# Attention and a gated feed-forward network on one core: pairs of logits emitted by free banks instead of fixed slots, other durations in the planner, and dense work dealt out differently

## The chip, the cores and the metric

The kernel runs on one NeuronCore of a Trainium2 chip. The core has a matrix engine (TensorE, "PE" in the profile), three engines for element-wise work (VectorE "DVE", ScalarE "ACT", GpSimd "POOL"), a queue engine (SyncE "SP") and 16 DMA engines. TensorE writes into PSUM, which has eight banks of 128 x 512 float32. The metric is the device time of one execution in microseconds.

## The reference

Two branches read the same input x (2048 tokens x 640) and are mixed by a gate that depends on the token:

```python
g = sigmoid((x * gate_w).sum(-1, keepdims=True))
out = g * A(x) + (1 - g) * B(x)
```

B is a feed-forward network, `(silu(x @ w1) * (x @ w3)) @ w2` with 1728 hidden columns. A is attention with a memory, 32 heads of 20 columns, the tokens in four chunks of 512:

```python
for s in range(4):                     # chunks
    logits = qs @ ks.T * scale + mask  # mask: (key > query) * -1e9
    a_dot = softmax(logits) @ vs
    a_mem = (phi(qs) @ M) / (phi(qs) @ z + 1e-6)
    o = sigmoid(beta) * a_mem + (1 - sigmoid(beta)) * a_dot
    M += phi(ks).T @ vs ; z += phi(ks).sum()
out_A = concat(o) @ wo
```

Everything is float32.

## The kernel before

**Precision.** A float32 operand is split into a high and a low part of type float32r (`split`, `parts`, `split_psum`), and three products (high x high, high x low, low x high; `PASSES`) stand for one. ScalarE makes the high part, VectorE or GpSimd the low part. A few small products (the memory's `pm` and `nd`, and the product of the probabilities with the values, `o`) use plain float32.

**Two halves of the array.** Nearly all matmuls use 64 of TensorE's 128 rows. `halves` cuts the 128-deep sum of a tile into a part for rows 0 to 63 (r = 0) and one for rows 64 to 127 (r = 1); while one tile does its first part on half 0, an older tile does its second part on half 1. Logits are made for two heads at once, one on each half.

**The planner.** The Python source writes the order of all engines by hand: an instruction runs on its engine in the order in which the source emits it. To choose this order the source keeps a clock of its own. `put(r, ns)` adds a matmul's duration to the clock of its half, `clocks[r]`; `go(engine, ns)` adds to that engine's time, `busy`; `until[bank]` is the time at which a PSUM bank is empty again. `stages` emits a chain of instructions on several engines, each when the one before is done by this clock. The durations are constants in the source: `COL` (0.4533 ns a column) for float32r matmuls, `COL4` for float32 ones, `MIN_MM` as a floor.

**Dense work.** A `Work` is one PSUM tile: its matmuls and the function that empties it (`evac`). Dense work is written as generators of `Work`: projections q, k and v; `ffn_up` (g and u), `ffn_down` (f, a sum over a group of three hidden blocks); the output projection (op); the memory (`pkt`, `pm`, `nd`); the normalisation of the attention's output (`rr`, `gt`). `step` emits one matmul, of the half whose clock is behind. `under` holds tiles on their first half, `behind_one` tiles that wait for their second, `flight` the one on it. `braid` runs one generator as a `Side` of another: it gives a tile every so many nanoseconds of dense work.

**Attention.** `attention()` walks through slots, 40 for a quad of heads (two pairs). `S_AT` and `T_AT` name the slots in which a pair's logits are made: `s_unit` makes them queries by keys for the row maxima (VectorE, L981), `max_rows` sends the maxima back into the operands by DMA, `t_unit` makes them again, transposed, with the maxima in, for the exponentials (ScalarE, L1026, into P) and masks (GpSimd, L1035). `pv_quad` multiplies P by the values (o, L1052); the last row of o is the sum of the probabilities. A unit takes two banks with `take_bank`; if none is free by the source's clock, the clock is moved on. `o_sums` and `o_scale` turn a chunk's sums into factors: one DMA brings them to `rs`, six VectorE instructions make reciprocals in three bfloat16 parts `rp`, six DMAs bring these into `rR`, and `rr` matmuls spread them over the output's rows.

**Segments.** `segs` lists dense jobs with the slot at which they must be done: 0 (the FFN of chunks 0 and 1, after the projections in `head`), 1, 2, 3 and 4. Within a segment the loop at the end of the kernel deals out dense work evenly over its slots. What remains after the last slot is `tail`: a down projection for group 3 of chunks 2 and 3, the last group, and the output projection of chunk 3.

## Time and profile before

| | us |
|---|---|
| median of 3 runs | 1137.55 (1133.83 to 1139.9) |
| the profiled execution's own time | 1137.45 |
| its span, first to last instruction | 1135.7 |
| TensorE busy | 1106.9 |
| VectorE, GpSimd, ScalarE busy | 582.5, 552.0, 485.6 |

The mean granted TensorE clock is 0.993. A row of the groups reads: line, engine, operation, out<-in by the program's names, partitions x elements, count, then busy time, mean duration in ns, and the idle time of the engine just before these instructions with what ended it. The names are those of the kernel: g, u, f, op, q, k, v are dense tiles; s and t the two kinds of logits; o the product with the values; P the probabilities; W and ht split weights and hidden blocks. "PE" rows are matmuls, "PEld" rows weight loads. A timeline row begins with its start and its duration in us, and ends with the idle time before it.

### The profile page before, as it was taken

To read this page: it belongs to the slowest core of one execution; us is meant where nothing else is said; L and a number is where in the kernel's file an instruction comes from. 1 tells how busy PE (TensorE), PEld (TensorE's weight loads), DVE (VectorE), ACT (ScalarE), POOL (GpSimd) and SP (SyncE) were. 2 spreads that over 40 slices of the span, in tenths; PEclk is the share of its full clock that TensorE was granted. 3 is DMA by queue.
4 is the path that set the end of the run, shared out by engine and by line. 5 is a ranking of instruction groups with operands and counts; after the bars stand their busy time and mean duration, and the time that the engine had idled before them with its cause. 6 is when DMAs were issued, how large, how long until landed. Compare 5 with 4: busy or idle time off the path is not lost. (4 is left out here: it accounts for less than half of the span.)

```text
span 1135.7 us, 29817 instructions
## 1 busy us (share of the span) xinstructions
PE 1106.9 (97%) x11798; PEld 988.7 (87%) x11798; DVE 582.5 (51%) x1735; ACT 485.6 (43%) x1003; POOL 552.0 (49%) x739
## 2 busy tenths in 40 slices
PE   9999999999999999999999989999999999999998
PEld 6999998988888998889989878888788888886998
DVE  6032564355555544473344666663457674652553
ACT  5255334543352433355456634535442445245130
POOL 5444356455464545334445445555663657464230
PEclk9999999999999999999999999999999999999999
DMA  7456753334343423614477863426533434452111
GB/s 258 149 195 223 250 153 95 88 93 113 90 115 91 105 54 98 197 48 140 158 257 244 270 212 94 122 84 194 152 99 93 121 95 116 119 142 65 41 67 62
DMA packets 85883, 152.34 MB, mean 134 GB/s; under 512 B 19914, under 2 KB 33009, under 8 KB 85745
## 3 DMA queue, kind: packets, MB, share of 16 engines
q1 hardware_dynamic: 55569, 94.13, 25.9%
q0 software_dynamic: 22976, 41.90, 15.3%
q10 hardware_dynamic: 7200, 14.42, 3.4%
q8 instruction: 93, 1.52, 0.6%
q14 instruction: 45, 0.37, 0.1%
HBM read 94.92 MB, written 54.53 MB: 132 GB/s over the span
## 5 line engine op out<-in xcount | busy, mean ns | idle before, releaser
L251 PE MATMUL g<-X,W 64*128 64x512 f32 x1680 | 390.9, 397 | 0.1
L251 PE MATMUL u<-X,W 64*128 64x512 f32 x1560 | 373.9, 397 | 0.0
L981 DVE CUSTOM_DVE_ANT_0 junk<-s,mask 128x128 bf16<-128x128 f32 (+3 forms) x512 | 250.9, 490 | 201.2 <-PE s L970 164.9
L1026 ACT ACTIVATE P<-t 128x384 f32<-128x384 f32 (+1 forms) x384 | 180.4, 526 | 247.4 <-PE t L1019 235.0
L251 PEld LDWEIGHTS g<-X,W 64*128 64x128 f32 x1680 | 271.9, 186 | 15.2 <-issue 2.0
L167 POOL TENSOR_TENSOR W<-wr,W 128x640 fp32r<-128x640 f32 (+1 forms) x125 | 195.3, 1569 | 162.6 <-ACT W L171 156.5
L251 PE MATMUL f<-W,ht 64*128 64x320 f32 x2624 | 268.3, 311 | 5.0 <-POOL ht L880 3.4
L251 PEld LDWEIGHTS u<-X,W 64*128 64x128 f32 x1560 | 259.0, 187 | 14.4 <-issue 1.8
L251 PEld LDWEIGHTS f<-W,ht 64*128 64x128 f32 x2624 | 249.2, 187 | 10.4 <-POOL ht L880 5.1
L1035 POOL TENSOR_SCALAR_AFFINE_SELECT P<-P 128x256 f32<-128x256 f32 (+1 forms) x192 | 94.4, 496 | 256.1 <-ACT P L1026 217.5
L171 ACT CAST W<-wr 128x640 fp32r<-128x640 f32 (+1 forms) x130 | 91.5, 727 | 49.2 <-PE f L251 20.5
L1019 PE MATMUL t<-qk 62*128 62x256 f32 (+2 forms) x512 | 99.6, 335 | 7.1 <-DVE m L981 4.6
L251 PE MATMUL op<-W,oT 64*128 64x320 f32 x960 | 99.6, 310 | 2.1 <-DVE oT L167 2.0
L970 PE MATMUL s<-qk 60*128 60x256 f32 (+2 forms) x512 | 94.5, 328 | 3.7 <-ACT P L1026 1.8
L918 DVE SCALAR_TENSOR_TENSOR acc<-f,cgate,acc 128x320 f32<-128x320 f32 x128 | 69.9, 549 | 52.7 <-PE f L251 52.2
L251 PE MATMUL k<-X,W 64*128 64x512 f32 x600 | 95.9, 397 | 0.4 <-SPq L254 0.4
L251 PEld LDWEIGHTS op<-W,oT 64*128 64x128 f32 x960 | 91.2, 186 | 4.3 <-DVE oT L167 3.4
L1006 POOL DMA_DIRECT2D qk<-mr x128 | 73.5, 576 | 35.7 <-DVE mr L1000 30.4
L880 POOL TENSOR_TENSOR ht<-ft,ht 128x512 fp32r<-128x512 f32 x52 | 67.1, 1289 | 48.5 <-ACT ht L884 41.6
L251 PE MATMUL q<-X,W 64*128 64x512 f32 x540 | 86.8, 395 | 0.0
L251 PE MATMUL v<-W,X 64*128 64x320 f32 (+1 forms) x960 | 82.8, 307 | 0.0
L251 PEld LDWEIGHTS k<-X,W 64*128 64x128 f32 x600 | 79.3, 185 | 3.3 <-SPq L254 1.1
(117 smaller groups left out, 1305.5 us busy)
## 6 DMA issues: line engine op xcount, KB each, us to landing
qk<-qkd POOLq DMA_DIRECT2D x128, 240.0 KB, 3.9
wr<-in_w_dram SPq DMA_DIRECT2D x80, 320.0 KB
qkd<-qs SPq DMA_DIRECT2D x20, 512.0 KB
qkd<-ks SPq DMA_DIRECT2D x20, 512.0 KB
od<-oq ACTq DMA_DIRECT2D x32, 256.0 KB
wr<-in_wo_dram SPq DMA_DIRECT2D x20, 320.0 KB
vg<-vd SPq DMA_DIRECT2D x16, 336.0 KB
xr<-in_xT_dram SPq DMA_DIRECT2D x20, 256.0 KB
```

What stands on the lines that cost most here:

```text
L167: (nc.vector if lo else nc.gpsimd).tensor_sub(dst[:, 1], src, dst[:, 0].bitcast(F32))
L171: stages(bank, ("act", ns, lambda: nc.scalar.copy(dst[:, 0], src)), ("dve" if lo else "pool", 1.1 * ns if lo else 2.2 * ns, low))
L251: ins = nc.tensor.matmul(o, l, x, start=i == 0 and (r == 0 or not w.todo[0]), stop=i == len(todo) - 1 and (r == 1 or not w.todo[1]), skip_ ...
L880: nc.gpsimd.tensor_sub(ht[:, 1], t, ht[:, 0].bitcast(F32))
L918: nc.vector.scalar_tensor_tensor(dst, ps[:, :320], cgate[:, c, lb:lb + 1], dst, op0=ALU.mult, op1=ALU.add)
L970: nc.tensor.matmul(ps[i][:, o:o + n], q[:, qb * P:(qb + 1) * P], k[:, :n], start=qb != 1, stop=qb != 0, skip_group_check=True)
L981: nc.vector.tensor_tensor_reduce(out=junk[:, :n], in0=ps[i][:, o:o + n], in1=mask[:, L - n:], scale=1.0, scalar=-3.0e38, op0=ALU.add, op1= ...
L1006: after(3 + 9 * k + a, lambda d=dst, r=r: here(nc.gpsimd.dma_start(d, mr[r:r + 8])))
L1019: nc.tensor.matmul(ps[i][:, o:o + L - q0], k[:, kb * P:(kb + 1) * P], q[:, q0:], start=kb != 2, stop=kb != 3, skip_group_check=True)
L1026: nc.scalar.activation(u["P"][:, i, o:o + n], ps[i][:, b:b + n], AF.Exp, scale=SCALE)
L1035: nc.gpsimd.affine_select(d, d, pattern=[[0, 2], [0, n], [1, P]], base=0, channel_multiplier=-1, compare_op=ALU.is_ge, fill=0.0)
```

## The change

`s_unit` and `t_unit` are no longer called in their slots. The slot puts them into a list `units`, and `events`, called after each dense matmul, takes the first from it when three banks are free by the source's clock, or two when the unit is more than `LATE` = 3 slots late; after 6 slots it is emitted anyway, and `flush` empties the list where something needs it. Side jobs open only with three free banks and VectorE's time less than 1 us ahead. A matmul of the second half may go before a new tile is opened when no bank is free, by up to `AHEAD`. Durations are changed, and GpSimd's DMA issues get 580 ns each (`ISSUE`). `o_scale` becomes a chain of stages. The output projection's tiles wait for the part of oT that they read. Dense jobs are moved between segments, and once the segments are used up the loop takes work from the tail.

```diff
-COL, COL4, MIN_MM, APART = 0.4533, 1.667, 110, 5
+COL, COL4, MIN_MM, APART, ISSUE, AHEAD = 0.4533, 0.85, 62, 5, 580, 1000
...
+LATE = 3
...
-               ("dve" if lo else "pool", 1.1 * ns if lo else 2.2 * ns, low))
+               ("dve" if lo else "pool", 1.4 * ns if lo else 2.15 * ns, low))
...
+    def free(n):
+        return sum(t <= now() for t in until) >= n
...
     def events():
 
         due()
+        if units and (free(3) or units[0][0] + LATE < clock["slot"] and free(2)):
+            unit()
...
-            elif dense["ns"] >= d.due and len(under) < 2 and len(behind_one) < 3:
+            elif dense["ns"] >= d.due and len(under) < 2 and len(behind_one) < 3 and free(3) and busy["dve"] < now() + 1000:
...
-        if flight[0] is not None and (clocks[1] < clocks[0] or run is None and not under and not waiting):
+        if flight[0] is not None and (clocks[1] < clocks[0] + (0 if under or free(1) else AHEAD)
+                                      or run is None and not under and not waiting):
...
             if not lower():
-                raise RuntimeError("nothing makes " + waiting[0].name + " ready")
+                if not heap:
+                    raise RuntimeError("nothing makes " + waiting[0].name + " ready")
+                force()
...
         queue.dma_start(raw[:, :n], src)
+        if queue is nc.gpsimd:
+            go("pool", ISSUE)
...
         while i not in tiles:
-            if i in halfway:
+            if i >= clock["oldest"] + NW:
+                if not lower():
+                    raise RuntimeError("no room for weight " + str(i))
+            elif i in halfway:
                 force()
...
-                until[bank] = go("act", 420 if hf == 0 else 700)
+                until[bank] = go("act", 430 if hf == 0 else 660)
...
+    def row_in(u, dst, src):
+        nc.gpsimd.dma_start(dst, src)
+        go("pool", ISSUE)
+        u["in"] = u.get("in", 0) + 1
...
     def max_rows(p):
 
+        flush(lambda: all(f is t_unit or q > p + 1 for _, f, q, _ in units))
         while min(pairs[p + k].get("rows", 0) for k in range(2)) < 6:
             force()
...
-                    after(3 + 9 * k + a, lambda d=dst, r=r: here(nc.gpsimd.dma_start(d, mr[r:r + 8])))
+                    after(3 + 9 * k + a, row_in, pairs[p + k], dst, mr[r:r + 8])
...
     def t_unit(p, t):
 
         u = pairs[p]
+        while u.get("in") != 2:
+            if not soon:
+                force()
+            tick()
...
-                go("pool", 500)
+                go("pool", 430 if n == 1 else 640)
...
     def o_scale(c):
 
-        here(nc.vector.reciprocal(rs, rs))
-        nc.vector.tensor_scalar(rs, rs, cR, None, op0=ALU.mult)
-        nc.vector.tensor_copy(rp[:, 0], rs)
-        nc.vector.tensor_sub(rs, rs, rp[:, 0])
-        nc.vector.tensor_copy(rp[:, 1], rs)
-        nc.vector.tensor_sub(rp[:, 2], rs, rp[:, 1])
-        go("dve", 2200)
-        end = c == NSEG - 1
-        for i in range(3):
+        def send(i):
             for k, (base, h0, n) in enumerate(((0, 0, R1H + 1), (64, R1H, H - R1H))):
                 dst = rR[base + n * i:base + n * i + n].rearrange("h (a n) -> h a n", n=P)
-                queue = nc.gpsimd if end and k else nc.sync
-                after(3 + 2 * i if end else 3 + 2 * i + k,
-                      lambda d=dst, s=rp[4 * h0:4 * h0 + 4 * n, i], q=queue: here(q.dma_start(d, s)))
-        after(11, turned.append, c)
+                queue = nc.gpsimd if k else nc.sync
+                after(1 + k, lambda d=dst, s=rp[4 * h0:4 * h0 + 4 * n, i], q=queue:
+                      (q.dma_start(d, s), q is nc.gpsimd and go("pool", ISSUE)))
+
+        def last():
+            send(2)
+            after(6, turned.append, c)
+
+        def keep(i):
+            return "dve", 240, lambda: nc.vector.tensor_copy(rp[:, i], rs)
+
+        def rest(i):
+            send(i)
+            nc.vector.tensor_sub(rs if i == 0 else rp[:, 2], rs, rp[:, i])
+
+        stages(None, ("dve", 950, lambda: nc.vector.reciprocal(rs, rs)),
+               ("dve", 320, lambda: nc.vector.tensor_scalar(rs, rs, cR, None, op0=ALU.mult)),
+               keep(0), ("dve", 300, lambda: rest(0)), keep(1), ("dve", 300, lambda: rest(1)), ("dve", 0, last))
...
+    def unit():
+
+        _, f, p, t = units.popleft()
+        even()
+        f(p, t)
+
+    def flush(ready):
+
+        while units and not ready():
+            unit()
+
     def attention():
...
-                even()
+                clock["slot"] += 1
                 if n == 2 and 0 <= m - 2 < NQUAD:
+                    flush(lambda: all(p > 2 * m - 3 for _, f, p, _ in units if f is t_unit))
+                    even()
                     pv_quad(2 * m - 4)
                 if n in S_AT and 0 <= m < NQUAD:
                     i, x = S_AT[n]
-                    s_unit(2 * m + i, x)
+                    units.append((clock["slot"], s_unit, 2 * m + i, x))
                 if n in T_AT and 0 <= m - 1 < NQUAD:
                     i, x = T_AT[n]
-                    t_unit(2 * m - 2 + i, x)
+                    units.append((clock["slot"], t_unit, 2 * m - 2 + i, x))
...
-                    load_pair(2 * (m + 1) + (n > 28))
+                    p = 2 * (m + 1) + (n > 28)
+                    flush(lambda: all(q % NST != p % NST for _, _, q, _ in units))
+                    load_pair(p)
+                if units and (units[0][0] + 2 * LATE < clock["slot"]):
+                    unit()
...
             def parts(ps):
-                assert qb in ready, (c, qb)
-                return halves([lambda kb=kb, a=a, b=b: (ps[:, :320], oT[0][:, qb % 2, a, kb * P:(kb + 1) * P],
+                def left(a, kb):
+                    while (qb, KB if kb > 1 else 2) not in ready:
+                        force()
+                    return oT[0][:, qb % 2, a, kb * P:(kb + 1) * P]
+
+                return halves([lambda kb=kb, a=a, b=b: (ps[:, :320], left(a, kb),
...
-            return Work(f"op{c}_{qb}_{hf}", parts, evac, plan[0], olds, lambda: qb in ready)
+            return Work(f"op{c}_{qb}_{hf}", parts, evac, plan[0], olds, lambda: (qb, 2) in ready)
...
-    seg += [braid(chain(g[:2]), job_read(1), 2500, 4000)] + g[2:] + jobs_group(A, 1) + jobs_up(A, 2)
-    segs.append((H + LAG + 1, seg))
-    d = job_down(A, 2)
-    u = [job_up(A, j, j == GROUPS[3][1]) for j in GROUPS[3][:2]]
+    seg += [braid(chain(g[:3]), job_read(1), 3600, 4000)] + g[3:] + jobs_group(A, 1) + jobs_up(A, 2) + [job_down(A, 2)]
+    seg += [job_up(A, j) for j in GROUPS[3][:2]]
+    segs.append((H + LAG + 3, seg))
+    u = job_up(A, GROUPS[3][2], True)
     o1, o2 = jobs_oproj(0)
-    seg = [d, braid(chain(u), o1, 2500), o2] + [job_up(A, j) for j in GROUPS[3][2:]] + [job_down(A, 3)]
+    seg = [braid(u, o1, 1200, 4000), o2, job_down(A, 3)]
...
-    segs.append((3 * H + LAG + 1, seg))
-    d = job_down(B, 1)
-    u = [job_up(B, j, j == GROUPS[2][1]) for j in GROUPS[2][:2]]
+    seg += [job_down(B, 1), job_up(B, GROUPS[2][0])]
+    segs.append((3 * H + LAG + 3, seg))
+    u = [job_up(B, j, j == GROUPS[2][2]) for j in GROUPS[2][1:]]
     o1, o2 = jobs_oproj(2)
-    seg = [d, braid(chain(u), o1, 1700), o2] + [job_up(B, j) for j in GROUPS[2][2:]]
-    seg += [job_down(B, 2), braid(chain(jobs_up(B, 3)), (0, load_memory(3)), 3500)]
+    seg = [braid(chain(u), o1, 1700, 2500), o2, job_down(B, 2), braid(chain(jobs_up(B, 3)), (0, load_memory(3)), 3500)]
+    seg += [job_down(B, 3)]
     segs.append((NJ + LAG, seg))
-    d, u = job_down(B, 3), [job_up(B, j, j < NF) for j in GROUPS[4]]
+    u = [job_up(B, j, j < NF) for j in GROUPS[4]]
     d2, d3 = jobs_down_by_chunk(B, 4)
     o1, o2 = jobs_oproj(3)
-    tail = [braid(chain([d] + u + [d2]), o1, 1500, 10500), alternate(o2, d3)]
+    tail = [braid(chain(u + [d2]), o1, 1500, 4000), alternate(o2, d3)]
...
+    last = (d for _, g in tail for d in g)
     run = begin()
     while run:
         if slots == run[0] * 10 + LEAD:
+            if run[1] is last:
+                break
...
             d = step(run[1])
             if d is None:
-                if not segs:
-                    break
-                run = begin()
+                run = begin() if segs else [run[0], last, run[2]]
                 continue
             credit -= d
     on_step.append(tick)
-    run = (d for _, g in tail for d in g)
-    while step(run) is not None:
+    while step(last) is not None:
         pass
```

The left-out lines are further durations of the same kind, and `go("pool", ISSUE)` behind GpSimd's other DMA issues.

More of the change, by code (lines that the diff above doesn't have):

```diff
@@ L320, in events @@
                         open_work(y)
-    on_step = []
+    on_step, units = [], deque()
     def follow():
@@ L346, in step @@
                 open_work(waiting.popleft())
-            w = under[-1]
-            if one(0, w):
+            w = under[-1] if under else None
+            if w is not None and one(0, w):
                 under.remove(w)
@@ L414, in set_oldest @@
         clock["oldest"] = max(clock["oldest"], min([k, *floors.values()]))
-    early, raws, clock = [], [], dict(step=0, oldest=0, next=0, raws=2)
+    early, raws, clock = [], [], dict(slot=0, step=0, oldest=0, next=0, raws=2)
     freed = [0, 0]
@@ L729, in gates_of @@
             def gates_of():
-                nc.vector.tensor_scalar(gate[:, c], gate[:, c], 1.0, None, op0=ALU.add)
-                nc.vector.reciprocal(gate[:, c], gate[:, c])
-                nc.vector.tensor_scalar(cgate[:, c], gate[:, c], -1.0, 1.0, op0=ALU.mult, op1=ALU.add)
-                go("dve", 300)
+                stages(None,
+                       ("dve", 140, lambda: nc.vector.tensor_scalar(gate[:, c], gate[:, c], 1.0, None, op0=ALU.add)),
+                       ("dve", 140, lambda: nc.vector.reciprocal(gate[:, c], gate[:, c])),
+                       ("dve", 140, lambda: nc.vector.tensor_scalar(cgate[:, c], gate[:, c], -1.0, 1.0, op0=ALU.mult, op1=ALU.add)))
             olds = {3 * kb + 2: iv[kb] + 1 for kb in range(KB)} if end and (lb, hf) == (3, 1) else None
@@ L883, in evac @@
                 stages(bank, ("dve", 690, lambda: nc.vector.scalar_tensor_tensor(t, u, 0.5, pu, op0=ALU.mult, op1=ALU.mult), True),
-                       ("act", 600, lambda: nc.scalar.copy(ht[:, 0], t)), ("pool", 1290, low))
+                       ("act", 620, lambda: nc.scalar.copy(ht[:, 0], t)), ("pool", 1290, low))
             return evac
@@ L913, in evac @@
                 dst = accs[c][:, lb, 320 * hf:320 * hf + 320]
-                until[bank] = go("act", 430) if first else go("dve", 545)
+                until[bank] = go("act", 530) if first else go("dve", 545)
                 if first:
@@ L1111, in load_memory @@
             here(nc.gpsimd.dma_start(gm[:, qb], gd[c][:, qb]))
+            go("pool", ISSUE)
             if qb == 3:
@@ L1221, in part @@
                 split(oT[0][:, qb % 2].rearrange("p a (b n) -> p a b n", n=P)[:, :, b0:b1],
-                      oall[c][:, b0:b1, qb * P:(qb + 1) * P], True, 160 * (b1 - b0), lambda b=b1: b == KB and ready.add(qb))
+                      oall[c][:, b0:b1, qb * P:(qb + 1) * P], True, (170 if b0 else 205) * (b1 - b0), lambda b=b1: ready.add((qb, b)))
         ready = set()
@@ L1269, in store @@
             here(nc.gpsimd.dma_start(o[:, qb], accs[c][:, qb]))
+            go("pool", ISSUE)
             yield 1
```

1 line of the change is left out of this document (added).

## Prediction

> **What bounds the kernel now.** I read the page first, then the groups by line, the waits, and the timeline at the longest waits. The page's first part and its costliest groups:
>
> ```profile
> PE 1106.9 (97%) x11798; PEld 988.7 (87%) x11798; DVE 582.5 (51%) x1735; ACT 485.6 (43%) x1003; POOL 552.0 (49%) x739
> L251 PE MATMUL g<-X,W 64*128 64x512 f32 x1680 | 390.9, 397 | 0.1
> L251 PE MATMUL u<-X,W 64*128 64x512 f32 x1560 | 373.9, 397 | 0.0
> L251 PE MATMUL f<-W,ht 64*128 64x320 f32 x2624 | 268.3, 311 | 5.0 <-POOL ht L880 3.4
> L1019 PE MATMUL t<-qk 62*128 62x256 f32 (+2 forms) x512 | 99.6, 335 | 7.1 <-DVE m L981 4.6
> L251 PE MATMUL op<-W,oT 64*128 64x320 f32 x960 | 99.6, 310 | 2.1 <-DVE oT L167 2.0
> L251 PE MATMUL k<-X,W 64*128 64x512 f32 x600 | 95.9, 397 | 0.4 <-SPq L254 0.4
> L970 PE MATMUL s<-qk 60*128 60x256 f32 (+2 forms) x512 | 94.5, 328 | 3.7 <-ACT P L1026 1.8
> L251 PE MATMUL q<-X,W 64*128 64x512 f32 x540 | 86.8, 395 | 0.0
> L251 PE MATMUL v<-W,X 64*128 64x320 f32 (+1 forms) x960 | 82.8, 307 | 0.0
> ```
>
> TensorE bounds it; the other engines are about half busy. But the 97% hides a reserve: a matmul here uses 64 of 128 rows, two run at a time, and while only one half of the array works the row still reads busy. The rate with both halves full comes from two undisturbed stretches, the first of the timeline, the second of the chain that ended last:
>
> ```profile
> 1079.67 1.43 PE L251 MATMUL g<-X,W 64*128 64x512 f32 x10
> ...
> 1111.01 2.21 PE op L251 x30
> 1113.21 0.73 PE f L251 x10
> ```
>
> Ten g start within 1.43 - 0.39 = 1.04 us, nine steps of 0.116 us; 40 matmuls of 320 columns take 2.94 us, 0.0735 us each. So 4380 matmuls of 512 columns (g, u, k, q) are 506 us, 4544 of 320 (f, op, v) are 334, and 1024 of s and t, 352 columns on average by the code, at 0.080 between the two rates, are 82. The 32 products o take 2.3 us each (a row below), 73. Small ones add an estimated 40. That is some 1035 of the span's 1135.7 us: about 100 us are not work, while TensorE shows only 1135.7 - 1106.9 = 28.8 us of idle. That 100 us is all that a reordering can reach. No matmul is added or removed by the change.
>
> **Part 1, logits that wait for free banks (units, LATE, free, AHEAD, the conditions on Side jobs).** The slots go; a pair s or t is emitted when the source's clock sees three free PSUM banks, or two after three slots. Before t both halves stand idle for 7.1 us and before s for 3.7. A wait of one half alone does not count there; it shows at most as idle time of the weight loads:
>
> ```profile
> L1019 PEld LDWEIGHTS t<-qk 62*128 62x128 f32 x512 | 66.0, 186 | 15.8 <-issue 5.0 <-ACT P L1026 1.6 <-PE t L1019 1.4
> L970 PEld LDWEIGHTS s<-qk 60*128 60x128 f32 x512 | 64.2, 186 | 10.4 <-ACT P L1026 2.7 <-PE s L970 1.5 <-PE u L251 0.9
> ```
>
> So these waits cost between 10.8 and 26.2 us, and 3.4 of it belong to part 2: 7.4 to 22.8 remain. I take 15, and 10 of it gained, since a unit forced by its lateness still waits. The gain lies between 0 and 22.8. What is late next: exponentials and masks, as a delayed t delays ScalarE's P and with it o; a slot later costs nothing while a quad of heads has 40 slots. What stands behind a waiting s or t on TensorE is everything, for both halves: dense tiles are queued in program order.
>
> **Part 2, the normaliser in pieces (o_scale, gates_of).** Six VectorE instructions were emitted in one block; now each is a stage, and others come between. The timeline shows what the block did at chunk 1 (VectorE, then TensorE):
>
> ```profile
> 676.42 1.65 DVE L1087 TENSOR_TENSOR rs<-rs,rp 128x128 f32<-128x128 f32 x1
> ...
> 679.00 0.42 DVE L981 CUSTOM_DVE_ANT_0 junk<-s,mask 128x256 bf16<-128x256 f32 x1
> ```
>
> ```profile
> 679.58 0.76 PE L1019 MATMUL t<-qk 62*128 62x256 f32 x3 [3.41 <-DVE m L981]
> ```
>
> Row maxima stood behind the block, no bank came free, and t waited 3.41 us: the longest wait of the run. A stage at a time, a maximum waits for one instruction of at most 1.65 us. After such waits the granted clock falls (windows; the column after the busy times is PEclk):
>
> ```profile
> 504.80:508.20 3.40, 3.40 (x30) 3.40 (x28) 1.10 (x2) 0.00 (x0) 2.68 (x4) 0.50 0.45 178
> 678.90:685.70 6.80, 6.12 (x31) 6.15 (x33) 4.56 (x18) 0.87 (x2) 1.68 (x3) 0.50 0.43 96
> 1044.10:1047.50 3.40, 3.40 (x26) 1.59 (x24) 0.00 (x0) 1.30 (x4) 1.38 (x3) 0.50 0.27 99
> ```
>
> At 0.50 the second stretch does 3.4 us of work in 6.8. Stall and clock together are worth 6.8; I take 6.5 (0 if the row maxima are still late, since rs comes by a DMA that nothing speeds up). The rR copies move: three of six per chunk now go out by GpSimd's queue for chunks 0 to 2 also. That is nine more issues, 0.576 us each by the row of L1006 below, 5.2 us on an engine at 49%, and nine fewer on SP; at nothing, while masks (P) behind them have slack, and 1.7 us at most for three in a row.
>
> **Part 3, the end of attention (last).** Before, dense work of the tail starts only after the last slot. Nothing dense runs in the last four microseconds before the last o (TensorE, then ScalarE):
>
> ```profile
> 1035.99 2.36 PE L1052 MATMUL o<-P,vg 128*32 128x512 f32 x32
> ...
> 1040.92 2.52 PE L1019 MATMUL t<-qk 62*128 62x512 f32 x8 [0.33 <-ACT P L1026]
> 1043.52 4.79 PE L1052 MATMUL o<-P,vg 128*32 128x512 f32 x32
> ```
>
> ```profile
> 1040.27 5.13 ACT L1026 ACTIVATE P<-t 128x512 f32<-128x512 f32 x12 [1.27 <-PE t L1019]
> ```
>
> Eight t at 0.080 are 0.64 us of work in 2.52: 1.9 lost; the last o takes 2.4 us more than the one before, at half clock. Sum 4.3. When the segment runs out, the changed loop takes tail work into these slots: 4 gained, between 0 and 4.3.
>
> **Part 4, measured durations and GpSimd's issues.** Here the source's clock was blind: a DMA issue occupies GpSimd, and the clock did not count it.
>
> ```profile
> L1006 POOL DMA_DIRECT2D qk<-mr x128 | 73.5, 576 | 35.7 <-DVE mr L1000 30.4
> 500.96 0.61 POOL L1269 DMA_DIRECT2D out_dram<-acc  x1
> 501.60 1.55 POOL L167 TENSOR_TENSOR W<-wr,W 128x642 fp32r<-128x642 f32 x1
> 503.10 1.27 POOL L880 TENSOR_TENSOR ht<-ft,ht 128x512 fp32r<-128x512 f32 x1
> ```
>
> ```profile
> 504.43 0.88 PE L251 MATMUL f<-W,ht 64*128 64x320 f32 x6 [2.25 <-POOL ht L880]
> ```
>
> The ht that f needs stood behind an issue and a weight split; f waited 2.25 us, and the clock was halved for 3.4 us, 1.7 more. All f waits are 5.0 us, with that clock 6.7. The order of GpSimd's work there stays much as it is, and a tile still counts as ready once its instruction is emitted: 3 gained, between 0 and 6.7. Of op's 2.1 us (oT late), 1 is gained by the longer durations; the finer readiness of oT lets op start earlier, which could also put a wait on the second part in its middle.
>
> One duration goes the other way. COL4 falls from 1.667 to 0.85 ns a column. The timeline of pm, one half of the array:
>
> ```profile
> 572.12 0.41 PE L251 MATMUL pm<-V,pkn 64*128 64x147 f32 x2
> 572.37 0.41 PE L251 MATMUL pm<-V,pkn 64*128 64x147 f32 x2
> ```
>
> Two records take 0.25 us, 0.125 each, so 0.85 ns a column is right for a record. But one float32 matmul of the source leaves two records: 15 pm tiles of 8 matmuls are 120, and the page counts 240 (nd 288 for 144). Per matmul 1.667 x 147 = 245 ns was right, and 0.85 x 147 = 125 ns is half. A half of a pm tile, four matmuls, is counted 0.5 us short, one of nd (2 x 147 and 84 columns) 0.32 us. If the other half then starves, and this one when the roles turn, 15 x 0.5 + 24 x 0.32 = 15.2 us are lost. If matmuls of the other half can go ahead, the two errors cancel: 0. Nothing in the trace tells program order from start order, and neither end is nearer by a row; nd and pm themselves have 1.0 us of idle at most, so dense neighbours absorb small skews: I take 4 lost. The floor for transposes, 110 to 62 ns, is worth under 240 x 0.048 / 2 = 5.8 us; I put it at nothing, as it covers itself in the same dense neighbours.
>
> The Trainium skill (TensorE: Matmul & The Clock Gate, Step-by-step: what each phase is for) says that only weight loads are pulled ahead and matmuls stay in program order. No row here shows which holds. By that page the term is 15.2 lost instead of 4, and the total comes out 11 us later; it is the third rival below.
>
> **Part 5, dense work shared out anew.** Two f_up jobs and a down job move from segment 1 to 0, a down and an up job from segment 4 to 3, and the down job of group 3 from the tail into segment 4. Attention's pace before (matmuls s per window):
>
> ```profile
> 345.00:600.00 255.00, 17.80 (x96) 0.99 0.42 126
> 825.00:1050.00 225.00, 26.46 (x138) 0.99 0.41 106
> ```
>
> 0.38 and 0.61 a microsecond; the shift evens this out, mostly in the first half. Work is the same; I put the evening at nothing beside part 1, +3 to -3. The tail loses 21.5 us of cover (8 x 2 tiles, 9 matmuls by two halves each 0.0735: 16 x 18 x 0.0735). In the tail of before:
>
> ```profile
> 1062.27 0.37 PE L251 MATMUL rr<-rR,sel 60*128 60x512 bf16 x1 [2.29 <-DMA rR<-rp]
> L251 PE MATMUL op<-W,oT x240: 299/307/411, 1104.5 to 1130.5; 64*128 64x320 f32 x120
> ```
>
> From the last o (1048.3) to rr 14 us pass, ten turns follow at 1.5 us, and oT takes 2: 31 us, and 2 less with the copies of rR sent as they come. The cover was 56 us and becomes 35 less what is drawn into attention's end, some 5: 30 against 29. I take 2 lost, 0 to 8. Side jobs held back by the new conditions come in a clump when their partner ends: 2 lost, 0 to 6.
>
> **Sum.** -10 - 6.5 - 4 - 3 - 1 + 4 + 2 + 2 = -16.5, on the profiled 1137.45 (span 1135.7 and 1.75 around it; the median of the runs is 1137.55, the same): 1121.
>
> **Rivals.** *Slower: units starve.* One or two tiles open, up to four behind and one in flight hold six of eight banks, so three free are rare; pairs go late, and the flush before o emits them in a row, as at 1040.92, where eight t lost 1.9 us to ScalarE. If one quad in three has such a burst, 11 x 1.9 = 21, and two clock drops of 1.7 add 3. Part 1 gives nothing: 1137.5 - 6.5 + 24 = 1155. It decides from 6.5 + 5.7 = 12 us, six bursts. Against it: VectorE and ScalarE are half idle, and a bank is held briefly. The three drops of the clock followed waits, so a new wait of 2 to 3 us is dear. 17%.
> *No change:* the waits change places; the total stays, 1137. For it speaks that no engine gets less work. 10%.
> *Program order:* COL4 costs 15.2, 1132. 10%.
> *Better:* waits of one half go too, part 1 at 22.8, parts 2 to 4 at their ends (6.8, 4.3, 6.7, 2), no new ones: -42.6, at the most 1095; I take 1100. For it: 100 us are not work. 13%.
>
> **How the numbers follow.** The forecast has 50%, with 1108 to 1130 of its own. The range must reach into the slower case and to the better one: 1099 to 1150. 0.5% is about what a measurement can tell from no change. Faster: 50 + 13 + half of program order 5 = 68%; within it 10 + 5 = 15%; slower 17%.
>
> **What would show it.** Part 1: idle before t and s under 5 us together (10.8 now). Part 2: no wait over 2 us near the second o_scale and no half clock there. Part 3: g, u or f between the last t. Part 4: f's idle near 2 us. COL4: dense groups beside pm and nd with gaps, and TensorE busy no lower though the span is longer. Tail: idle before rr and op. Wrong if t, s or o wait in bursts, or the granted clock falls more than three times.

## The result, and the profile after

The changed kernel is slower: 1150.22 us (median of 4 runs, 1149.42 to 1151.51) against 1136.39 for the kernel before, a ratio of 1.0121 [1.009, 1.0151]. I had forecast 1121, faster. The profiled execution of the changed kernel took 1149.42 us, its span is 1147.6 and its mean granted clock 0.987 (before: 1137.45, 1135.7, 0.993).

The page of the changed kernel, first part and four of the costliest groups (what ends a row is the idle time before these matmuls and what ended most of it):

```profile
PE 1120.1 (98%) x11798; PEld 1002.1 (87%) x11798; DVE 586.3 (51%) x1735; ACT 486.9 (42%) x1003; POOL 557.1 (49%) x748
...
L255 PE MATMUL f<-W,ht 64*128 64x320 f32 x2624 | 269.2, 310 | 9.8 <-ACT acc L930 2.9
...
L255 PE MATMUL op<-W,oT 64*128 64x320 f32 x960 | 109.1, 328 | 7.6 <-ACT oT L172 5.5
...
L1044 PE MATMUL t<-qk 62*128 62x256 f32 (+2 forms) x512 | 94.3, 328 | 1.9 <-ACT P L1051 1.5
...
L985 PE MATMUL s<-qk 60*128 60x256 f32 (+2 forms) x512 | 94.6, 331 | 0.3
```

The waits before s and t did go, from 10.8 to 2.2 us. In their place stand f (5.0 to 9.8) and op (2.1 to 7.6). TensorE's idle time as a whole is 1147.6 - 1120.1 = 27.5 us, against 28.8: it is not longer, and yet the kernel is. So the loss has to be looked for where the page says busy. The windows of the changed kernel (span of the window; busy time of PE, PEld, DVE, ACT, POOL; then the granted clock, the DMA share and GB/s):

```profile
718.39:721.80 3.41, 1.53 (x20) 1.20 (x18) 3.41 (x7) 1.02 (x2) 1.27 (x1) 1.00 0.56 173
721.80:732.00 10.20, 9.63 (x53) 8.95 (x53) 4.43 (x18) 2.93 (x6) 1.97 (x2) 0.50 0.00 0
...
783.30:786.70 3.40, 0.75 (x12) 0.48 (x8) 1.47 (x8) 0.31 (x1) 0.00 (x0) 0.99 0.41 150
786.70:790.10 3.40, 3.13 (x22) 3.03 (x24) 0.00 (x0) 3.00 (x7) 0.00 (x0) 0.50 0.23 82
...
936.90:940.30 3.40, 0.77 (x10) 0.63 (x9) 3.26 (x9) 1.02 (x2) 1.26 (x1) 0.99 0.00 0
940.30:950.50 10.20, 9.92 (x57) 9.52 (x58) 4.04 (x14) 2.72 (x6) 1.54 (x1) 0.50 0.01 2
...
1114.40:1117.80 3.40, 2.08 (x12) 1.82 (x13) 3.16 (x7) 1.64 (x4) 0.00 (x0) 0.99 0.24 96
1117.80:1121.20 3.40, 3.40 (x23) 3.40 (x23) 0.02 (x1) 0.00 (x0) 0.00 (x0) 0.51 0.00 0
```

27.2 us at half clock up to the last matmul, against 13.6 before. Three of the four stretches begin where op waits for oT, the transposed output of attention; the other begins where f waits 2.92 us for acc (its row stands further below). TensorE and then VectorE and ScalarE around the first of them:

```profile
717.62 1.41 PE L253 MATMUL gt<-ident,gm 64*128 64x64 f32 x20
...
718.87 0.35 PE L253 MATMUL gt<-ident,gm 64*128 64x64 f32 x3
...
721.39 0.57 PE L255 MATMUL op<-W,oT 64*128 64x320 f32 x2 [1.88 <-ACT oT L172]
722.44 2.68 PE L255 MATMUL op<-W,oT 64*128 64x320 f32 x7 [0.48 <-DVE oT L168]
```

```profile
718.98 3.07 DVE L1178 TENSOR_TENSOR oall<-oall,gt 128x512 f32<-128x512 f32 x5
721.97 0.42 DVE L168 TENSOR_TENSOR oT<-oall,oT 128x256 fp32r<-128x256 f32 x1
```

```profile
720.93 0.40 ACT L172 CAST oT<-oall 128x256 fp32r<-128x256 f32 x1 [1.81 <-DVE oall L1178]
```

The last products of the normalisation (gt) come in a row, VectorE needs 3.07 us for the five additions behind them, oT follows, and op, which is next on TensorE, waits. In the kernel before the same products are spread out, and op starts 10 us after the last of them (TensorE, before):

```profile
698.62 0.28 PE L249 MATMUL gt<-ident,gm 64*128 64x64 f32 x2
...
711.09 0.22 PE L249 MATMUL gt<-ident,gm 64*128 64x64 f32 x1
...
721.01 0.30 PE L251 MATMUL op<-W,oT 64*128 64x320 f32 x1
```

**A measure for all runs.** Each run lists its span and mean granted clock. (1 - clock) x span is about what the clock cost; the remainder is about the span that the same order would have at full clock. An estimate, as the clock has three decimals (0.6 us a run), and as every profiled run also shows half clock behind its last matmul, for 2 to 5 us (4.9 before, 4.7 after, 3.9 in e18), where nothing is lost: 1 to 2.5 us of each cost, and in e18 all of it. The columns are means over a kernel's runs. One execution of e23, 1335.73 us at a granted clock of 0.752, is left out of its row.

| kernel | median us | ratio to before [95%] | clock's cost | remainder |
|---|---|---|---|---|
| before | 1135.2 | 1 | 7.6 | 1126.2 |
| after | 1150.2 | 1.0121 [1.009, 1.0151] | 15.5 | 1133.0 |
| e1_side_old | 1136.5 | 1.0007 [0.9989, 1.0025] | 9.0 | 1125.6 |
| e10_free_only | 1152.5 | 1.0147 [1.012, 1.0175] | 16.4 | 1134.5 |
| e15_banks_only | 1153.0 | 1.016 [1.0131, 1.0189] | 18.4 | 1132.7 |
| e7_before_side | 1139.4 | 1.0035 [1.0016, 1.0054] | 12.1 | 1125.5 |
| e2_share_old | 1144.5 | 1.0086 [1.0054, 1.0118] | 11.2 | 1132.4 |
| e3_side_share_old | 1138.5 | 1.0022 [1.0005, 1.0039] | 7.0 | 1129.7 |
| e4_ready_old | 1150.7 | 1.0132 [1.01, 1.0165] | 16.7 | 1131.8 |
| e9_slots | 1133.6 | 0.998 [0.9964, 0.9996] | 10.5 | 1121.2 |
| e16_slots_limit | 1133.9 | 0.9985 [0.9962, 1.0007] | 9.6 | 1122.4 |
| e19_slots_tail | 1127.4 | 0.994 [0.992, 0.9961] | 5.1 | 1120.7 |
| e18_slots_share_old | 1123.7 | 0.9904 [0.9875, 0.9932] | 1.4 | 1120.7 |
| e22_slots_share_col4 | 1122.9 | 0.9885 [0.9863, 0.9906] | 3.9 | 1117.2 |
| e23_slots_share_noissue | 1124.8 | 0.9912 [0.9886, 0.9939] | 2.5 | 1120.7 |
| e5_side_col4 | 1139.6 | 1.0044 [1.0027, 1.0062] | 8.5 | 1129.0 |
| e6_before_oscale | 1135.2 | 1.0 [0.9981, 1.002] | 9.9 | 1124.2 |
| e8_side_tail_old | 1141.4 | 1.0048 [1.0032, 1.0064] | 7.3 | 1131.9 |
| e12_flush | 1136.3 | 0.9998 [0.998, 1.0016] | 8.4 | 1125.4 |
| e14_order | 1136.4 | 1.0012 [0.9995, 1.0028] | 9.6 | 1125.2 |

Of the loss about half is the clock (7.6 to 15.5) and half the remainder (1126.2 to 1133.0). The first row's median is over all runs of the kernel before, the ratios go by those beside each kernel. Below, differences between kernels are of medians; where they ran beside other executions of the kernel before, the ratios give up to 2 us more or less (e9 to e18: 8.6 instead of 9.9; e9 to e19: 4.5 instead of 6.2; e1 to e5: 4.2 instead of 3.1).

### The profile page after: what moved, and what is told of

It is laid out like the page before. It is cut to its first block, busy times and chain, and to the rows that moved or that the text cites. A ratio compares the mean times of both kernels' runs of the same rounds, so it can differ in the third digit from the quotient of the medians.

```text
span 1147.6 us, 29862 instructions
## 1 busy us (share of the span) xinstructions
PE 1120.1 (98%) x11798; PEld 1002.1 (87%) x11798; DVE 586.3 (51%) x1735; ACT 486.9 (42%) x1003; POOL 557.1 (49%) x748
## 3 DMA queue, kind: packets, MB, share of 16 engines
q0 software_dynamic: 23264, 42.02, 15.2%
## 4 chain that ended last, share of the span: by engine, by line
PE 88%; DVE 3%; POOL 3%; issue 2%; ACT 1%; DMA 1%; SPq 1%; DVEq 0%; POOLq 0%; ACTq 0%
PE g L255 16%; PE f L255 16%; PE u L255 15%; PE op L255 6%; PE o L1077 6%; PE v L255 6%; PE k L255 6%; PE q L255 6%; PE s L985 4%; PE t L1044 3%; PE nd L255 2%; PE pm L255 1%; DVE junk L996 1%; POOL W L168 1%; DVE oall L1178 1%
## 5 line engine op out<-in xcount | busy, mean ns | idle before, releaser
L255 PE MATMUL g<-X,W 64*128 64x512 f32 x1680 | 380.7, 394 | 0.1
L255 PE MATMUL u<-X,W 64*128 64x512 f32 x1560 | 366.6, 394 | 0.0
L255 PEld LDWEIGHTS g<-X,W 64*128 64x128 f32 x1680 | 265.6, 185 | 16.5 <-issue 1.5
L255 PEld LDWEIGHTS u<-X,W 64*128 64x128 f32 x1560 | 256.3, 185 | 17.0 <-issue 2.2
L255 PEld LDWEIGHTS f<-W,ht 64*128 64x128 f32 x2624 | 249.0, 187 | 15.2 <-POOL ht L894 3.5
L255 PE MATMUL op<-W,oT 64*128 64x320 f32 x960 | 109.1, 328 | 7.6 <-ACT oT L172 5.5
L255 PEld LDWEIGHTS op<-W,oT 64*128 64x128 f32 x960 | 99.6, 200 | 11.4 <-ACT oT L172 6.0
L1044 PE MATMUL t<-qk 62*128 62x256 f32 (+2 forms) x512 | 94.3, 328 | 1.9 <-ACT P L1051 1.5
L962 POOL DMA_DIRECT2D qk<-qkd x128 | 70.0, 551 | 44.9 <-PE t L1044 34.8
```

Source lines behind the costliest of these rows:

```text
L255: ins = nc.tensor.matmul(o, l, x, start=i == 0 and (r == 0 or not w.todo[0]), stop=i == len(todo) - 1 and (r == 1 or not w.todo[1]), skip_ ...
L962: here(nc.gpsimd.dma_start(t[64 * i:64 * i + RH], qkd[c][RH * (h + i):RH * (h + i + 1)]))
L1044: nc.tensor.matmul(ps[i][:, o:o + L - q0], k[:, kb * P:(kb + 1) * P], q[:, q0:], start=kb != 2, stop=kb != 3, skip_group_check=True)
```

## The experiments

Five edits can be undone one by one: the condition on Side jobs, the new shares of dense work, op's readiness, the waiting of units, and durations. "Units" are the waiting pairs of logits, "slots" the fixed ones.

**Side jobs, shares, readiness.** Four kernels, from the changed one:

```diff
-            elif dense["ns"] >= d.due and len(under) < 2 and len(behind_one) < 3 and free(3) and busy["dve"] < now() + 1000:
+            elif dense["ns"] >= d.due and len(under) < 2 and len(behind_one) < 3:
```

> The changed kernel, with the old condition for Side jobs (no three free banks, no VectorE limit). Side theory (the new conditions hold back the normalisation's tiles gt until their partner work is over, so that they come in one row, oT is late, and op waits): idle before op falls from 7.6 to about 2.5 us, half clock from 27 to about 10 us, time 1132. Share theory (the dense work left beside the normalisation is too short): op still waits, time 1145 to 1150.

e1: 1136.46. 13.8 us of the loss hang on this line: 6.5 of the clock and 7.4 of the remainder. op's idle time falls as the Side theory had it (the page of e1):

```profile
L255 PE MATMUL op<-W,oT 64*128 64x320 f32 x960 | 109.6, 320 | 3.4 <-DVE oT L168 2.0
```

The two stretches of 10.2 us at half clock behind op are gone; some 17 us at half clock remain up to the last matmul, where that theory had 10. The next puts back the segments and the tail of before (in short; all of `segs` between is as before too), e3 does both:

```diff
-    seg = [braid(u, o1, 1200, 4000), o2, job_down(A, 3)]
+    seg = [d, braid(chain(u), o1, 2500), o2] + [job_up(A, j) for j in GROUPS[3][2:]] + [job_down(A, 3)]
...
-    seg += [job_down(B, 3)]
...
-    tail = [braid(chain(u + [d2]), o1, 1500, 4000), alternate(o2, d3)]
+    tail = [braid(chain([d] + u + [d2]), o1, 1500, 10500), alternate(o2, d3)]
```

> The changed kernel, with the old distribution of dense jobs over segments and tail. Share theory: op's and f's waits for oT and W go (f9 and f2_6 waited 3.8 and 2.6 us for W right behind op), time 1134. Side theory: the waits for W go (6 us), the wait of op of chunk 1, whose partner work is not touched, stays; time 1143.

> Both undone: units, durations, o_scale and readiness stay. Side and share theories both: 1122 to 1128, under the kernel before, for idle before t and s stays near 2 us. If the loss lies in the units or in the durations (COL4): not under 1140.

e2: 1144.48, e3: 1138.48. With the new condition the old shares are 5.7 us better, without it 2.0 worse: the two edits are not independent, and without the condition the new shares look harmless up to here. e4 makes op ready only with the whole oT:

```diff
-                      ... lambda b=b1: ready.add((qb, b)))
+                      ... lambda b=b1: ready.update([(qb, 2), (qb, KB)]) if b == KB else None)
```

> The changed kernel, but op counts as ready only when the whole oT of its rows has been emitted. Side and share theories: op is late all the same, 1147 to 1151. Readiness theory (op is begun too early and blocks both halves of the array): idle before op falls by more than half, time 1140.

e4: 1150.65, as the changed kernel. That op may start on a part of oT is not the cause.

**Which half of the condition?** e10 keeps VectorE's limit and drops the three banks (its label names the other half); e15 keeps the banks and drops the limit.

```diff
-   ... and len(behind_one) < 3 and free(3) and busy["dve"] < now() + 1000:
+   ... and len(behind_one) < 3 and busy["dve"] < now() + 1000:     (e10)
+   ... and len(behind_one) < 3 and free(3):                        (e15)
```

> The changed kernel (1150) with one half of the new Side condition dropped: three free banks are no longer asked, VectorE's limit stays. If the banks are the half that starves the Side jobs: 1134 to 1140, as without the whole condition. If it is VectorE's limit: 1147 to 1152.

> The changed kernel (1150) with the other half of the Side condition dropped: three free banks are asked, VectorE's limit of 1 us is gone. If VectorE's limit is what starves the normalisation: 1134 to 1140 and idle before op under 5 us. If either half is enough to starve it: 1147 to 1152.

1152.48 and 1152.97: either half alone costs as much as both. The waits of op in e15:

```profile
PE op L255 <- DVE oT L168: 5.2, 5, 2.1
...
PE op L255 <- ACT oT L172: 3.7, 3, 1.5
```

So not one threshold is to blame; something makes any such condition fail. e7 puts the condition alone into the kernel before (with `free`, and `force()` where nothing else makes a tile ready), e16 into the changed kernel with fixed slots, that is with every unit counted as late and emitted in the slot that lists it:

```diff
-LATE = 3
+LATE = -1
```

> The kernel before with the new condition for Side jobs alone. Side theory: op waits for oT behind a row of gt tiles, half clock rises from 14 us, 1146 to 1156. If the condition hurts only together with waiting units (which hold banks longer): 1135 to 1140.

> The changed kernel, with both halves of the Side condition, but every unit in its slot (LATE -1). If the condition costs 14 us by itself with the new shares: 1146 to 1152. If it costs that only where units wait as well: 1135 to 1141, as in the kernel before with the condition.

e7: 1139.35, some 4 us over the kernel before beside it (1134.75). e16: 1133.92, against 1133.60 for the same kernel without the condition (e9, next). With slots it costs nothing here: that the 13.8 us need units and condition both is measured. Why is only argued from the code: `events` calls a waiting unit as soon as three banks are free, and it takes two of them, so the Side job that asks for three (in e15) comes after it. In e10 no banks are asked for; there, units emitted when banks fall free would bring their row maxima to VectorE, which would fail the limit of 1 us. The trace of e16 goes against this as the whole account, for the gt come in a row there too, without waiting units. At chunk 1 an o of 2.3 us follows them and op waits for nothing (TensorE):

```profile
712.48 1.40 PE L253 MATMUL gt<-ident,gm 64*128 64x64 f32 x20
713.81 2.36 PE L1077 MATMUL o<-P,vg 128*32 128x512 f32 x32
716.10 1.20 PE L255 MATMUL op<-W,oT 64*128 64x320 f32 x4
```

At chunks 2 and 3 nothing lies between, and op does wait, 1.40 and 1.74 us (the waits of op in e16: total, times, longest):

```profile
PE op L255 <- ACT oT L172: 3.1, 2, 1.7
```

So the condition puts the gt in rows with slots as well; what a row costs at one chunk goes by what stands between it and op, and the clock's cost of e16 as a whole is no higher than that of e9 (9.6 and 10.5). What makes the condition so dear beside waiting units is not settled by these runs.

**Units or slots?** e9 is e1 with `LATE = -1`, e18 is e3 with it.

> The kernel of e1_side_old (1136.5 us) with every unit emitted in its slot (LATE -1); durations, shares, o_scale, readiness stay. If waiting for free banks is worth what the waits before t and s show: idle before t and s rises from under 2.5 to about 10 us, the waits of o for masks fall, 1143 to 1147. If units only move waits: 1133 to 1139.

> Slots, old Side condition and old shares: of the change only durations, GpSimd's issues, o_scale, the readiness of op and the tail's work in the last slots stay. Against e9_slots (1133.6) it shows what the new shares are worth: if they gain as the even pace should, 1137 to 1142 here; if they cost op and f their cover, 1127 to 1131.

e9: 1133.60, e18: 1123.74, 1% faster than the kernel before. Idle time before t and s in e9 (its page):

```profile
L1044 PE MATMUL t<-qk 62*128 62x256 f32 (+2 forms) x512 | 100.2, 328 | 0.6 <-DVE gm L695 0.2
...
L985 PE MATMUL s<-qk 60*128 60x256 f32 (+2 forms) x512 | 96.1, 326 | 0.0
```

With fixed slots these waits are gone as well: it was not the waiting for free banks that took them away. Which of the other edits did is not tested. Units cost 2.9 us with the new shares (e1 over e9) and 14.7 with the old ones (e3 over e18). The table orders this: the remainder rises by 4.4 and 9.0, and the clock does the rest, -1.5 and +5.6. With the new shares, what rises is partly seen in the waits of e1 (total, times, longest), as e9 shows no wait of o; with the old ones it is less clear, as e3 has 3.7 us of these waits and e18 2.4:

```profile
PE o L1077 <- POOL P L1060: 4.4, 2, 3.2
```

and on GpSimd in e1, before the longest of them:

```profile
892.67 1.27 POOL L894 TENSOR_TENSOR ht<-ft,ht 128x512 fp32r<-128x512 f32 x1
893.88 0.61 POOL L1114 DMA_DIRECT2D rR<-rp  x1
894.51 1.02 POOL L1060 TENSOR_SCALAR_AFFINE_SELECT P<-P 128x256 f32<-128x256 f32 x2
```

The masks of the quad stand behind a hidden block's split and a copy of rR, and o for them. Two kernels on that. e12 empties the list of late t units four slots before o, e14 puts a down job between normalisation and op (in short; the same at chunk 2):

```diff
+                if n == 38 and 0 <= m - 1 < NQUAD:
+                    flush(lambda: all(f is s_unit for _, f, _, _ in units))
```

> The kernel of e1_side_old; all late t units of a quad are emitted four slots before its o instead of right before it. Late-unit theory (o waits for masks, 4.4 us in two waits, because flush emits the last t just before o): no wait of o over 0.5 us, half clock 3.4 us less, 1130 to 1134. If the t units then wait for banks: 1136 to 1139.

```diff
-    seg = [braid(u, o1, 1200, 4000), o2, job_down(A, 3)]
+    seg = [braid(chain([u, d]), o1, 1700, 4000), o2]
```

> The kernel of e1_side_old with the down jobs of group 3 (chunks 0 and 1) and group 2 (chunks 2 and 3) between the normalisation and op instead of behind op. Cover theory (op's place in the order is too early for oT, and f's right behind op too early for its W): waits of op at chunks 0 and 2 and of f9 and f2_6 for W go, 6 to 9 us, 1127 to 1131. If the weights are late anyway: the waits for W stand before op, 1135 to 1138.

1136.29 and 1136.39, both as e1. In e12 TensorE's order is that of e1 (but for neighbours that start together): no t unit was that late, so late units do not make o wait. In e14 the waits of f changed from the split of W to ht, and op now waits 2.2 us for W, as its second expectation had it. Why units cost the remainder 4 to 9 us is settled no further than this.

**The shares again, with slots.** e18 and e9 differ in the shares alone: 9.9 us. e19 is e9 with the down job of group 3 back in the tail, e8 the same on e1:

```diff
-    seg += [job_down(B, 3)]
...
-    tail = [braid(chain(u + [d2]), o1, 1500, 4000), alternate(o2, d3)]
+    tail = [braid(chain([d] + u + [d2]), o1, 1500, 10500), alternate(o2, d3)]
```

> The kernel of e9_slots with the down job of group 3 back in the tail. In e9 op of chunk 3 waits 2.4 us, the other half of the array 6.0, and 6.8 us behind it run at half clock. Cover theory: 1127 to 1130. If the time goes elsewhere, as in e8_side_tail_old: 1134 to 1139.

> The kernel of e1_side_old with the down job of group 3 back in the tail, segments otherwise as changed. Cover theory (the tail is too short for the normalisation of the last chunk; op of chunk 3 waited 5 us and 6.8 us ran at half clock): 1128 to 1131, no wait over 1 us before that op. If the wait moves elsewhere: 1135.

e19: 1127.38, 6.2 us better than e9. e8: 1141.42, 5.0 worse than e1; with units the job in the tail gave longer waits of o for its masks instead (7.5 us in all, 4.4 in e1). The remainders of e9, e19 and e18 are the same to half a microsecond (1121.2, 1120.7, 1120.7), their clock's cost is 10.5, 5.1 and 1.4: **by this estimate, with slots the new shares cost clock and nothing else.** The end of e9 (windows as above) around op of chunk 3, and then of e19:

```profile
1094.60:1098.00 3.40, 2.35 (x35) 2.06 (x33) 3.23 (x7) 0.05 (x1) 0.00 (x0) 1.00 0.51 199
1098.00:1101.40 3.40, 2.50 (x12) 2.24 (x13) 2.77 (x6) 1.59 (x4) 0.00 (x0) 0.86 0.00 0
1101.40:1104.80 3.40, 3.40 (x22) 3.40 (x23) 0.00 (x0) 0.00 (x0) 0.00 (x0) 0.50 0.00 0
1104.80:1108.20 3.40, 3.40 (x33) 3.40 (x32) 0.55 (x1) 0.00 (x0) 0.00 (x0) 0.63 0.00 0
```

```profile
1095.00:1098.40 3.40, 3.39 (x41) 3.12 (x37) 2.37 (x5) 0.00 (x0) 0.26 (x1) 1.00 0.60 239
1098.40:1101.80 3.40, 3.23 (x44) 3.23 (x46) 0.55 (x1) 0.00 (x0) 0.00 (x0) 1.00 0.24 96
```

Without that down job the tail has too little to do while oT is made; 1.95 us of idle time in two windows are followed by three windows below full clock, which cost (0.14 + 0.50 + 0.37) x 3.4 = 3.4 us more. e18, with the old shares, keeps full clock through op of chunk 1 (its window, and its rows of f and op on the page):

```profile
720.00:733.00 13.00, 12.98 (x158) 11.85 (x162) 10.09 (x27) 5.81 (x14) 9.40 (x14) 1.00 0.46 120
```

```profile
L255 PE MATMUL f<-W,ht 64*128 64x320 f32 x2624 | 265.0, 308 | 2.3 <-POOL ht L894 1.4
...
L255 PE MATMUL op<-W,oT 64*128 64x320 f32 x960 | 97.9, 310 | 3.1 <-DVE oT L168 2.9
```

**COL4 and GpSimd's issues.** Each undone in e18 (e22, e23), COL4 in e1 also (e5); -60 makes `go` add nothing for an issue.

```diff
-COL, COL4, MIN_MM, APART, ISSUE, AHEAD = 0.4533, 0.85, 62, 5, 580, 1000
+COL, COL4, MIN_MM, APART, ISSUE, AHEAD = 0.4533, 1.667, 62, 5, 580, 1000    (e5, e22)
+COL, COL4, MIN_MM, APART, ISSUE, AHEAD = 0.4533, 0.85, 62, 5, -60, 1000     (e23)
```

> The kernel of e1_side_old (1136.5 us) with COL4 back at 1.667, so that a float32 matmul counts both of its records; the transposes' 62 ns stay. Starvation theory (half the duration makes the other half of the array wait): up to 15 us less, 1121 to 1130, and less idle beside pm and nd. Absorption theory (the errors of the two halves cancel): 1134 to 1139, no change outside the noise.

> The kernel of e18_slots_share_old (1123.7, under the kernel before) with COL4 back at 1.667. Starvation theory: up to 15 us less, 1109 to 1119, gaps of the dense groups beside nd and pm go. Absorption theory: 1121 to 1127.

> The kernel of e18_slots_share_old with GpSimd's DMA issues out of the source's clock again (ISSUE adds nothing). If knowing the 162 us of issues is what brings the gain over the kernel before: 1130 to 1135, f waits for ht and W again. If the gain is o_scale's and the tail's: 1122 to 1126.

e5: 1139.59, 3.1 us over e1. e22: 1122.88, 0.9 under e18, and with a ratio of 0.9885 [0.9863, 0.9906] the fastest of the study. e23: 1124.8, 1.1 over e18, the intervals overlapping. The right value of COL4 gains nothing in e1 and one to two microseconds in e18, within what the runs can tell; by the table the remainder rises by 3.4 in the one and falls by 3.5 in the other, where the clock takes 2.5 of it back; counting the issues gains less than can be told.

**o_scale alone.** e6 puts the normaliser in stages into the kernel before (in short; with the early sending of rR's parts, and with `force()` as in e7).

```diff
-        go("dve", 2200)
+        stages(None, ("dve", 950, lambda: nc.vector.reciprocal(rs, rs)),
+               ("dve", 320, lambda: nc.vector.tensor_scalar(rs, rs, cR, None, op0=ALU.mult)),
+               keep(0), ("dve", 300, lambda: rest(0)), keep(1), ("dve", 300, lambda: rest(1)), ("dve", 0, last))
```

> The kernel before with o_scale in stages alone. Block theory (the six instructions in one block hold back row maxima): the wait of 3.4 us before t near 676 us and the half clock behind it go, 1130 +- 3. If the wait comes from rs landing late or from something else there: a wait of 2 us or more stays near it, 1136 +- 3.

e6: 1135.18 against 1134.75, no gain. The wait of 3.41 us before t is gone, but TensorE shows a new one of 3.23 us before f at 1055.96 and one before op at chunk 2, and behind the latter the windows show a new stretch of half clock:

```profile
899.88 0.87 PE L249 MATMUL gt<-ident,gm 64*128 64x64 f32 x18
...
906.33 0.56 PE L251 MATMUL op<-W,oT 64*128 64x320 f32 x2 [1.24 <-ACT oT L171]
```

```profile
907.80:911.20 3.40, 3.40 (x15) 2.09 (x19) 1.08 (x3) 0.00 (x0) 0.64 (x2) 0.50 0.03 3
```

By the table the remainder falls by 2.0 and the clock's cost rises by 2.3.

## Why the prediction was wrong, step by step

**Side jobs held back (+2, 0 to 6): the step that failed.** It measured +13.8 in the changed kernel (e1). I costed the condition by itself, and by itself it is in that range: some 4 on the kernel before (e7), 0.3 with slots (e16). Beside waiting units it leaves the last gt close before op, and op waits for oT (7.6 us in all, 3.4 without the condition) with 20 us at half clock behind two of these waits. That a unit takes the banks for which the Side job waits, which I did not work out, may be a part of it; e10, which asks for no banks, and the rows of gt in e16 say that it is not the whole. My slower rival had units that starve, and put the late work on t; what starved was the normalisation, and op waited. The rival's 1155 is near 1150, its mechanism is not the one: idle time before t is 1.9 us.

**Part 1, units (-10, 0 to -22.8): wrong in sign.** The sign that I named came out (2.2 us before s and t, under 5), but e9 has it without units. Priced with everything else as it is, they cost 2.9 (new shares) or 14.7 (old). The term was sized by idle time in front of s and t, and taking that away does not shorten a kernel whose idle time reappears before o, f and op.

**Part 5, shares (0, within 3) and tail (+2, 0 to 8): too small.** With slots they cost 9.9, of which 6.2 lie in the tail, inside its range, and 3.7 in the other shares, outside theirs (by the ratios 4.5 and 4.1). I compared the tail's cover in microseconds of work and found it enough by one (the cover lost is 21.2 by the factors that I gave, not 21.5, which changes nothing); what decides is whether TensorE waits near op at all, since the clock then adds its own price: in e9 3.4 us to some 2 of waiting. The new shares also put a down job right behind op, whose weights were not split in time (TensorE, changed kernel):

```profile
441.99 0.41 PE L255 MATMUL f<-W,ht 64*128 64x320 f32 x1 [0.81 <-ACT W L172]
...
443.61 0.41 PE L255 MATMUL f<-W,ht 64*128 64x320 f32 x1 [1.21 <-POOL W L168]
...
786.97 1.43 PE L255 MATMUL f<-W,ht 64*128 64x320 f32 x8 [2.92 <-ACT acc L930]
```

The third row is the Side condition again, I think: e1 has no wait for acc, and in the changed kernel the output of an earlier chunk, whose store is a Side job, leaves late and holds its buffer.

**Part 2 (-6.5, 0 to -6.8): the stall went, the gain did not come** (e6: 0, the end of the range). That nothing else would be late next was the error. That the rR copies on GpSimd cost nothing was a little too kind: one stands right before the late masks shown for e1.

**Part 3 (-4, 0 to -4.3): the sign came, in the changed kernel not by this mechanism.** Its last slots (TensorE) have f before and behind the last o, which runs at full clock, 2.36 us against 4.79. But these f are the down job that part 5 moved into segment 4: the changed tail begins with g, and only two of its g start before the last o (the first at 1077.84). In e18, whose tail begins with that down job, f stands before the last t from 1034.73 on, so there the tail's work was drawn in as I had it. The term was not measured by itself.

```profile
1075.08 0.40 PE L1044 MATMUL t<-qk 62*128 62x256 f32 x4
1075.32 2.83 PE L255 MATMUL f<-W,ht 64*128 64x320 f32 x35
...
1078.52 2.36 PE L1077 MATMUL o<-P,vg 128*32 128x512 f32 x32
```

**Part 4 (-3 and -1).** In the changed kernel f's idle time rose to 9.8; in e18 it is 2.3, the "near 2" that I named. It is not the counting of GpSimd's issues that did it, as f's idle time is 2.3 in e23 too; which of the edits that e18 keeps did is open. **COL4 (+4, 0 to 15.2)** is at its zero end: e22 gains 0.9 by undoing it, e5 loses. The 15.2 that undoing it would have gained if the halves waited for each other came in no run: dense neighbours absorb the skew, or the two errors cancel; the runs don't tell these apart. The Trainium skill (TensorE: Matmul & The Clock Gate, Step-by-step: what each phase is for) has matmuls stay in program order. No run here shows whether they did.

**Parts 2 to 4 together** were -6.5 - 4 - 3 - 1 + 4 = -10.5; e18, which keeps these (and `AHEAD` and a few small waits of the planner), measures 1123.74 - 1134.69 = -10.95. The sum holds, though one of its terms (o_scale alone) does not, so I don't take it as a proof of the others. The forecast failed by its parts 1 and 5 and the Side term: -10 + 0 + 2 + 2 = -6, and 1150.22 - 1123.74 = +26.5 (24.6 by the ratios). Of the signs that would make it wrong, "the granted clock falls more than three times" is the one that came, with four falls.

## What to carry to other kernels

In an order written by a planner, price each new condition together with the other edits that act on the same resources: here it cost 13.8 us beside waiting units, and 0.3 or 4.6 without them. Judge a schedule by two numbers, the clock's cost and the remainder, not by idle time: the six fixed-slot orders made from the changed kernel lay some 5 us apart in the remainder and 9 in the clock. And before taking a wait away, name what will be at the head of TensorE's queue then; here it was op, whose input needs 3 us of VectorE after the last transpose.

## What the runs showed of the hardware

The clock halves after stretches in which TensorE still worked: 1.53 us of 3.41 (718.39 to 721.80 in the changed kernel) and even 2.08 of 3.40 (1114.40 to 1117.80). The Trainium skill (TensorE: Matmul & The Clock Gate, Part 1: The HAM clock gate) has it halve after an idle window of about 3.4 us and recover after a busy one. Here a partly idle one was enough, and half clock lasted 10.2 us twice, with TensorE busy for 9.63 and 9.92 of it by the profile, which counts a matmul on one half of the array as busy; the measurement decides. A wait of 2.4 us before op thus cost about 5 us more by the clock. In e18, where no wait behind the start was longer than 1.7 us (one t for a DMA), the clock stayed full up to the last matmul.

The runs of one kernel differ by it too: the shortest of the kernel before (1131.52) had 0.996, the longest (1143.52) 0.990, which is 0.006 x 1136 = 6.8 of their 12 us.
